# Attention over packed keys and a token-mixing MLP: new routes for the first loads, and a new order

## The chip, the cores and the metric

The kernel runs on one core of a Trainium2 chip. The metric is the device time of one execution in microseconds (us). The core has five engines that work side by side, each through its own list of instructions in order: TensorE (PE, with its weight loads as PEld), VectorE (DVE), ScalarE (ACT), GpSimd (POOL) and SyncE (SP). Transfers between the main memory (DRAM) and the on-chip memory run on 16 DMA engines. Three instruction lists hand out transfers here: SP and ACT feed hardware queues, which copy bytes as they are; GpSimd feeds a software queue, which can also cast float32 to bfloat16 on the way (the casting queue).

## The reference

Inputs: q, k, v of shape (8 batches, 8 heads, 576 tokens, 64), p of shape (8, 8, 32, 64), and three weights of the MLP; all float32.

```python
def sm_attn(qq, kk, vv):
    s = scale * np.matmul(qq, kk.transpose(0, 1, 3, 2))
    s = s - np.max(s, axis=-1, keepdims=True)
    a = np.exp(s)
    a = a / (np.sum(a, axis=-1, keepdims=True) + 1e-09)
    return np.matmul(a, vv)
p_packed = sm_attn(p, k, v)              # 32 packed tokens attend to 576
x = sm_attn(q, p_packed, p_packed)       # 576 tokens attend to 32; heads side by side: (8, 576, 512)
wq, wk = x @ w_q, x @ w_k                # 512 -> 64
W_tok = scale2 * einsum('bsd,btd->bst', wq, wk)
mixed = einsum('bst,btd->bsd', W_tok, x)
out = np.maximum(mixed, 0.0) @ w_out     # (8, 576, 512), float32
```

## The kernel before

The eight batches are independent, and each goes through the same steps. The order of all steps is one text, ORDER (lines 12 to 57): a list of items that a loop at the end of the kernel (line 599) turns into instructions one after the other. An item names a step, the batch, a part of it, after @ the engine (V, A, P for VectorE, ScalarE, GpSimd; S for SP), and after = the banks of the matmul memory. Since every engine runs its own instructions in the order in which they were issued, this text sets for each engine what stands behind what. Waits between engines follow from the data.

The steps of a batch b, in the order in which the data goes through them:

- LD.k, LD.v, LD.q (function load, line 154): the inputs, cast to bf16 on the casting queue. v is two requests (line 173), the others one (lines 176 and 182), q of batches 0 and 7 two halves, r and q (line 179). There are four buffers of each.
- KT (line 255): VectorE's 32 x 32 block transpose of k. S1 (line 263): scores of p against k on TensorE. X1 (line 293): their exponential on ScalarE. TE: a block transpose of that. PV (line 306): times v, 36 matmuls. RC, PP, PT: the division, a mask for the heads, and a transpose, on VectorE.
- QK, QKE, QD: the packed tokens times the small weights (wqk), copied out, and a copy on GpSimd.
- QV: the block transpose of q. S2 (line 373): scores of q against the packed tokens, in parts of the tokens (part 2 is the last 128-token piece, 0 and 1 pairs of pieces, 3 all four). X2 (line 378): exponential. HA (only batch 5, line 388): a first halving of the row sums on GpSimd. RS, RR, AM (lines 394, 399, 405): row sums, reciprocals, and the product on GpSimd (now and then VectorE). AT, AE: transposes on TensorE and their copies.
- WKQ, WE, GM, GE, Y, YE, MX, MR: the token mixing as a chain of matmuls and copies. RL, RLF, RLR: relu. OT (line 540): the output product, four matmuls each; OE, OEF: copies to the output tiles; ST, STF, STH: stores. OT.b.4 is a remainder of two batches together. OH, OEH, STH handle the last piece of batch 7 in halves.

WARM items (line 615) are matmuls on zeros whose results nobody reads. They stand in the first part of the order, the last ahead of MX.1.0 behind the scores S2.2 of batch 2. WARM.n is n units of 128 columns; a third number caps the width of each.

What the change touches stands at the start. p comes as two float32 copies, LD.N0 on ACT's queue and LD.N1 on SP's (line 161), into p32, and is cast by two ScalarE copies, NC (line 239), into pbf. PX (line 246) then transposes it into pT, which S1 of every batch reads. The two small weights come as LD.W0 and LD.W1 (line 164) behind p on the same hardware queues into w32, and GpSimd casts them, WC (line 243). On the casting queue k of batch 0 stands first, in halves: LD.h (line 168) and LD.g (line 157), then v, r, q of batch 0 and k1. SET items prepare constants: the mask, the identity (aff on GpSimd, idb), the ones beside v, the zeros beside aT.

HOLD.v7 (line 567) is a tiny copy on SP's queue which waits until v of batch 7 has landed; the stores on SP stand behind it. GpSimd gives out a few stores itself (ST items with @P).

Of the kernel before, what the change touches and what calls it, by code (L numbers as in the profile page):

```python
# [17 lines left out]
AM.0.2@P WARM.6=7 AT.0.2=7 AE.0.2@A RS.0.0@V RR.0.0@V KT.1.2@V WARM.5=6 S1.1=2,3,0,1 X1.1.0@A AM.0.0@P
RS.0.1@V AT.0.0=6 RR.0.1@V AE.0.0@V TE.1.0@V QD.0@P WARM.2=4 WKQ.0.0=4,5 WKQ.0.2 X1.1.1@A TE.1.1@V AM.0.1@P
AT.0.1=7 LD.q2 PV.1.0=2,3 PV.1.1 WE.0.0@V RC.1@V AE.0.1@A WKQ.0.1 WE.0.1@A WARM.2=6 GM.0=6 LD.k3 PP.1.1@V  # L20
PP.1.0@V PT.1@V QV.1.2@V GE.0@A WARM.1=0 Y.0=0,1 YE.0@A QK.1=4 QKE.1@V WARM.1=7 S2.1.2=2,3 S2.1.1=6,7 X2.1.2@A
RS.1.2@V S2.1.0=0,1 X2.1.1@A LD.O MR.0=4,5 RR.1.2@V AM.1.2@P RLR.0@A KT.2.2@V MX.0.1=2,3 WARM.3=6 AT.1.2=6
X2.1.0@A QD.1@P WARM.1=7 S1.2=4,5,0,1 RL.0.1@A LD.v3 AE.1.2@A MX.0.0=2,3 X1.2.1@A RS.1.0@V RR.1.0@V RS.1.1@V
AM.1.0@P X1.2.0@A TE.2.1@V RR.1.1@V AM.1.1@P TE.2.0@V RL.0.0@A WARM.6=7 AT.1.0=7 AE.1.0@V PV.2.0=0,1 PV.2.1
LD.k4 RC.2@V PP.2.0@V AT.1.1=6 AE.1.1@A LD.q3 LD.v4 WKQ.1.0=4,5 WKQ.1.2 WE.1.0@A PP.2.1@V WKQ.1.1 WE.1.1@A
PT.2@V QK.2=2 QKE.2@A QV.2.2@V LD.q4 WARM.1=3 GM.1=3 QD.2@P GE.1@A WARM.1=7 Y.1=6,7 S2.2.2=0,1 X2.2.2@A
KT.3.2@V S2.2.3=4,5 YE.1@A WARM.1=2 MX.1.0=2,3 X2.2.3@A MX.1.1=0,1 MR.1=6,7 RLR.1@A RS.2.4@V RL.1.0@A RR.2.4@V
# [33 lines left out]
def kernel(  # L61
# [92 lines left out]
    def load(x, eng):  # L154
        a, b = x[0], x[1:]
        if a == "g":
            nc.gpsimd.dma_start(k_in[0][:, 1], pairs(k, 0)[:, 1])
        elif a == "N":
            i, n = int(b), L * Dh // 4
            src = p.rearrange("b (i c) (z l) d -> i (c z) b (l d)", i=2, z=4)  # L160
            (nc.sync if eng == "S" else nc.scalar).dma_start(p32[:, i * n:(i + 1) * n], src[i])
        elif a == "W":
            w = (moe_w_k, moe_w_q)[int(b)].rearrange("(i c j e) m -> (c j) i (e m)", i=2, c=4, e=2)
            (nc.sync if eng == "S" else nc.scalar).dma_start(w32[:, int(b)], w)
        elif a == "O":
            nc.gpsimd.dma_start(wout, moe_w_out.rearrange("(j a) n -> a j n", a=P))
        elif a == "h":
            nc.gpsimd.dma_start(k_in[0][:, 0], pairs(k, 0)[:, 0])
        elif a == "v":
            b = int(b)  # L170
            for i in range(2):
                src = v[b, 4 * i:4 * i + 4].rearrange("c (g r) d -> g c (r d)", r=R)
                nc.gpsimd.dma_start(v_bufs[b % NL][halves(i), 0:7:2], src)  # L173
        elif a == "k":
            b = int(b)
            nc.gpsimd.dma_start(k_in[b % NL], pairs(k, b))
        elif a == "r" or x in ("q0", "q7"):
            b, i = int(b), int(a == "q")
            nc.gpsimd.dma_start(q_in[b % NL][:, i], pairs(q, b)[:, i])
        else:  # L180
            b = int(b)
            nc.gpsimd.dma_start(q_in[b % NL], pairs(q, b))
# [53 lines left out]
    def blocks(o, i):  # L236
        nc.vector.transpose(o, i)  # L237
# [411 lines left out]
```

## Time and profile before

| what | us |
|---|---|
| median of 3 runs (104.53 to 105.03) | 104.9 |
| the profiled execution | 105.18 |
| its span, first to last instruction | 103.4 |
| TensorE busy | 93.2 |
| VectorE busy | 74.0 |
| ScalarE busy | 65.2 |
| GpSimd busy | 53.2 |

A page of the profile gives busy times and groups of instructions by line of the kernel; out<-in are the names of the tiles. Some tiles share memory at the start: p32, pbf, w32 and the warm tile all appear as "o". The timeline gives start, duration, engine, line, operation, and in brackets how long the engine had stood idle before it, and which engine, line or DMA ended that. The chain of waits gives start, duration and work of the chain that ended last. The granted TensorE clock was 1.000 throughout.

### The profile page before, as it was taken

What the parts mean: (1) busy time and instruction counts of PE and PEld (TensorE: products, weight loads), DVE (VectorE), ACT (ScalarE), POOL (GpSimd) and SP (SyncE); (2) the same over time, 40 slices, a digit from 0 to 9 for tenths busy, and PEclk for the clock granted to TensorE, in tenths of its full rate; (3) what the DMA queues carried; (4) which work ended last, traced back from release to release, by engine and by line L of the source; (5) the groups of instructions that cost most, each with busy time, mean ns of one, the idle gap of its engine ahead of it and who ended that gap; (6) DMA issues with size and microseconds to landing.
All of it is one profiled execution on the core that took longest, in us unless ns stands there. A gap on an engine that the chain in (4) does not pass through costs nothing.

```text
span 103.4 us, 3594 instructions
## 1 busy us (share of the span) xinstructions
PE 93.2 (90%) x1531; PEld 57.3 (55%) x1546; DVE 74.0 (72%) x139; ACT 65.2 (63%) x112; POOL 53.2 (51%) x83
## 2 busy tenths in 40 slices
PE   5996999999979988999988899999999999999950
PEld 3895455567537744664547445684557763744430
DVE  4055366979597869696999959989899898138540
ACT  1340406164866697367975979899999698587320
POOL 5973890693379725943049289507667408200000
PEclk9999999999999999999999999999999999999999
DMA  1999999999999999999999999999999999965994
GB/s 27 233 229 207 213 210 206 210 213 209 209 213 209 207 209 211 213 210 209 213 208 210 216 207 206 213 210 210 208 314 406 413 422 403 410 266 227 388 361 163
DMA packets 13632, 25.13 MB, mean 243 GB/s; under 512 B 1073, under 2 KB 6449, under 8 KB 13617
## 3 DMA queue, kind: packets, MB, share of 16 engines
q0 software_dynamic: 10000, 17.30, 84.3%
q1 hardware_dynamic: 3056, 7.08, 18.0%
q10 hardware_dynamic: 560, 0.52, 2.0%
q8 instruction: 12, 0.20, 0.7%
q14 instruction: 4, 0.02, 0.1%
HBM read 30.15 MB, written 9.44 MB: 383 GB/s over the span
## 4 chain that ended last, share of the span: by engine, by line
PE 54%; DMA 22%; DVE 6%; ACT 6%; POOL 5%; issue 2%; SPq 1%; ACTq 0%; DVEq 0%; POOLq 0%
PE ps L540 27%; DMA k_sb<-in_k_dram 14%; DMA o<-in_moe_w_q_dram 8%; PE ps L315 4%; PE ps L373 3%; PE ps L419 3%; PE ps L446 3%; DVE kT L237 3%; ACT e L378 2%; PE ps L492 2%; PE ps L467 2%; PE ps L441 2%; POOL a L405 2%; PE ps L615 2%; PE ps L282 2%
## 5 line engine op out<-in xcount | busy, mean ns | idle before, releaser
L405 POOL TENSOR_TENSOR a<-e,rr 128x256 bf16<-128x256 f32 (+2 forms) x18 | 19.6, 1098 | 24.1 <-DVE rr L399 16.9
L540 PE MATMUL ps<-wout,relu 128*128 128x512 bf16 x112 | 29.2, 380 | 1.0 <-issue 0.5
L615 PE MATMUL ps<-o 128*128 128x128 f32 (+3 forms) x86 | 22.2, 397 | 1.3 <-DVE o L135 1.2
L540 PEld LDWEIGHTS <-relu 128*128 128x128 bf16 x124 | 10.6, 98 | 12.0 <-issue 1.8
L615 PEld LDWEIGHTS ps<-o 128*128 128x128 f32 x86 | 13.2, 213 | 6.0 <-issue 3.9
L128 ACT ACTIVATE o<-ps 128x1024 f32<-128x1024 f32 (+1 forms) x13 | 12.5, 959 | 4.2 <-PE ps L540 3.9
L293 ACT ACTIVATE e1T<-ps 128x576 bf16<-128x576 f32 x16 | 9.7, 653 | 7.2 <-PE ps L282 7.2
L394 DVE TENSOR_REDUCE rs<-e 128x16 f32<-128x512 f32 (+2 forms) x13 | 11.0, 850 | 2.9 <-ACT e L378 2.8
L378 ACT ACTIVATE e<-ps 128x256 f32<-128x256 f32 (+2 forms) x19 | 11.3, 625 | 2.3 <-PE ps L373 2.2
L237 DVE STREAM_TRANSPOSE kT<-k_sb 128x1152 uint32<-128x1152 uint32 (+1 forms) x9 | 11.0, 1218 | 2.1 <-DMA k_sb<-in_k_dram 2.1
L503 ACT ACTIVATE relu<-ps 128x1024 bf16<-128x1024 f32 (+1 forms) x12 | 11.1, 957 | 1.3 <-PE ps L492 1.2
L237 DVE STREAM_TRANSPOSE qT<-q_sb 128x1152 uint32<-128x1152 uint32 (+1 forms) x10 | 11.0, 1108 | 0.7 <-DMA q_sb<-in_q_dram 0.7
L173 POOL DMA_DIRECT2D v_sb<-in_v_dram x16 | 10.2, 648 | 0.3 <-POOL v_sb L206 0.3
L128 ACT ACTIVATE aT<-ps 128x128 bf16<-128x128 f32 (+2 forms) x12 | 6.4, 548 | 5.8 <-PE ps L419 4.4
L237 DVE STREAM_TRANSPOSE e<-e1T 128x288 uint32<-128x288 uint32 x16 | 7.1, 458 | 1.6 <-ACT e1T L293 1.3
L315 PE MATMUL ps<-v_sb,e 64*64 64x192 bf16 x288 | 7.5, 245 | 0.0
L128 ACT ACTIVATE wkq<-ps 128x448 bf16<-128x448 f32 (+1 forms) x8 | 5.8, 728 | 2.3 <-PE ps L446 1.4
L132 DVE COPY o<-ps 128x512 f32<-128x512 f32 (+2 forms) x7 | 5.4, 768 | 2.6 <-PE ps L540 1.9
L446 PE MATMUL ps<-aT,pqk 128*128 128x256 bf16 (+1 forms) x48 | 6.8, 246 | 0.0
L315 PEld LDWEIGHTS <-e 64*64 64x64 bf16 x288 | 5.9, 107 | 1.3 <-DVE e L237 0.9
L373 PE MATMUL ps<-ppT,qT 64*128 64x64 bf16 x320 | 6.5, 190 | 0.0
L441 PE MATMUL ps<-pqk,aT 128*128 128x64 bf16 x80 | 6.2, 194 | 0.3 <-ACT aT L128 0.2
(69 smaller groups left out, 134.5 us busy)
## 6 DMA issues: line engine op xcount, KB each, us to landing
v_sb<-in_v_dram POOLq DMA_DIRECT2D x16, 288.0 KB, 11.2
out_dram<-o SPq DMA_DIRECT2D x8, 512.0 KB, 6.5
k_sb<-in_k_dram POOLq DMA_DIRECT2D x7, 576.0 KB, 12.9
q_sb<-in_q_dram POOLq DMA_DIRECT2D x6, 576.0 KB, 13.3
out_dram<-o POOLq DMA_DIRECT2D x5, 512.0 KB, 9.1
out_dram<-o SPq DMA_DIRECT2D x5, 256.0 KB, 2.4
q_sb<-in_q_dram POOLq DMA_DIRECT2D x4, 288.0 KB, 11.3
out_dram<-orem SPq DMA_DIRECT2D x4, 256.0 KB, 6.1
```

The source lines that it names most:

```text
L128: nc.scalar.activation(o, i, COPY)
L173: nc.gpsimd.dma_start(v_bufs[b % NL][halves(i), 0:7:2], src)
L237: nc.vector.transpose(o, i)
L293: nc.scalar.activation(e1T[:, x], T["s1", b][x].rearrange("a c m -> a m c"), EXP, scale=scale)
L315: nc.tensor.matmul(T["pv", b][halves(cc), i], lhsT, rhs, start=n == 0, stop=n == R - 1, skip_group_check=True)
L378: nc.scalar.activation(e2[:, t0:t1].rearrange("a t (i y n) -> a y (t i) n", i=2, y=2), T["s2", b, c].rearrange("a y t i n -> a y (t i) n") ...
L394: nc.vector.tensor_reduce(rs[:, t0 * H:t1 * H], src, axis=AX, op=ADD)
L405: e.tensor_tensor(a2[:, t0:t1].rearrange("a t i (u l) -> a (t i u) l", l=L), e2v(b, c), T["rr", b][:, t0 * H:t1 * H].to_broadcast((P, (t1 ...
L446: nc.tensor.matmul(o, pqk[:, i, Dl:], aT[:, i, c0:c1], start=i == 0, stop=i == 1)
L503: nc.scalar.activation(o, i, RELU)
L540: nc.tensor.matmul(ps, lhsT, wout[:, j, :], start=j == 0, stop=j == NJ - 1)
L615: nc.tensor.matmul(bank(int(bk), [w]), warm[:, 0:P], rhs, start=True, stop=True)
```

## The change

- k of batch 0: the first half (LD.h, casting queue) becomes LD.H, a float32 copy on SP's hardware queue into h32 (in an output tile not yet in use), and a ScalarE copy HC casts it into k_in. The second half, LD.g, stays on the casting queue.
- p: LD.N0 and LD.N1 move to the head of the casting queue and land in bf16 in pbf. NC goes.
- The small weights: LD.W0 and LD.W1 move to the casting queue, W0 behind q and r of batch 0, W1 behind k1. WC goes.
- The mask is set on VectorE instead of GpSimd.
- ORDER is new from end to end. The requests of the casting queue were h g v0 r0 q0 k1 v1 q1 k2 v2 q2 k3 O v3 k4 q3 v4 q4 k5 v5 k6 q5 v6 q6 k7 v7 q7 r7 (O is w_out) and become N0 N1 g v0 q0 r0 W0 k1 W1 k2 v1 q1 v2 q2 O k3 v3 k4 q3 v4 q4 k5 v5 q5 k6 v6 q6 k7 v7 q7 r7. The last WARM stands ahead of QK.2. GpSimd's stores go from five (0.0, 1.1, 3.1, 4.1, 3.0) to two (1.1, 3.1), the others go on SP's queue.

```diff
 ORDER = """
-LD.N0@A LD.N1@S SET.warm@V SET.v0@V SET.aT0@V SET.aT1@V SET.aT2@V SET.idf@V LD.W0@A LD.W1@S SET.tab@A LD.h0
-LD.g0 LD.v0 LD.r0 LD.q0 LD.k1 NC.1@A PX.1@V NC.0@A PX.0@V SET.aff@P SET.idb@V KT.0.0@V KT.0.1@V SET.mask@P
-WARM.4=0 WARM.22.128=0 S1.0=0,1,2,3 X1.0.1@A TE.0.1@V X1.0.0@A TE.0.0@V SET.v2@P WARM.8=4 PV.0.0=4,5 PV.0.1
-RC.0@V PP.0.0@V PP.0.1@V PT.0@V WC.0@P QV.0.0@V WC.1@P WARM.6=6 QK.0=6 SET.v3@P QV.0.1@V QKE.0@A WARM.4=7
...
+LD.H@S SET.warm@V SET.v0@V SET.aT0@V SET.aT1@V SET.aT2@V SET.idf@V SET.tab@A LD.N0 LD.N1 LD.g0 LD.v0 LD.q0
+LD.r0 LD.W0 LD.k1 SET.aff@P SET.mask@V HC@A PX.0@V KT.0.0@V PX.1@V KT.0.1@V SET.idb@V WARM.4=0 WARM.18.128=0
+S1.0=0,1,2,3 X1.0.0@A TE.0.0@V X1.0.1@A TE.0.1@V WARM.8=4 PV.0.0=4,5 PV.0.1 RC.0@V PP.0.1@V PP.0.0@V QV.0.1@V
+PT.0@V LD.W1 QV.0.0@V WARM.12=6 S2.0.2=6,7 S2.0.0=0,1 X2.0.2@A RS.0.2@V RR.0.2@V LD.k2 SET.v1@P LD.v1
+S2.0.1=2,3 LD.q1 X2.0.0@A RS.0.0@V AM.0.2@P WARM.6=5 AT.0.2=5 X2.0.1@A RR.0.0@V AM.0.0@P WARM.5=4 AT.0.0=4
+AE.0.2@A AE.0.0@A RS.0.1@V RR.0.1@V AM.0.1@P QK.0=6 QKE.0@A KT.1.2@V QD.0@P S1.1=0,1,2,3 AT.0.1=7 WKQ.0.0=4,5
+X1.1.1@A WKQ.0.2 X1.1.0@A AE.0.1@V WKQ.0.1 TE.1.1@V WE.0.0@A WE.0.1@A WARM.3=6 GM.0=6 SET.v2@P GE.0@A WARM.1=2
+Y.0=2,3 YE.0@A TE.1.0@V KT.2.2@V S1.2=0,1,4,5 X1.2.0@A MR.0=6,7 RLR.0@V MX.0.1=2,3 MX.0.0=0,1 RL.0.1@V
+X1.2.1@A TE.2.1@V PV.1.0=6,7 PV.1.1 RC.1@V PP.1.0@V PP.1.1@V RL.0.0@A LD.v2 PT.1@V WARM.7=4 QK.1=4 LD.q2
+QKE.1@A QV.1.2@V WARM.4=5 S2.1.2=2,3 X2.1.2@A S2.1.0=0,1 S2.1.1=6,7 LD.O LD.k3 SET.v3@P X2.1.0@A TE.2.0@V
+WARM.5=5 PV.2.0=4,5 PV.2.1 LD.v3 LD.k4 RS.1.2@V RR.1.2@V RS.1.0@V QD.1@P AM.1.2@P AT.1.2=2 RR.1.0@V AM.1.0@P
...
+RC.4@V RR.3.4@V AM.3.3@P PP.4.0@V OT.2.1 OE.1.0@A PP.4.1@V PT.4@V QK.4=3 QV.4.2@V AM.3.2@P QKE.4@V AT.3.3=2
...
+AT.4.2=7 AE.4.2@A MR.3=4,5 RLR.3@A QV.5.2@V PT.5@V MX.3.1=0,1 RL.3.1@A MX.3.0=6,7 RL.3.0@A AT.4.3=3 OT.3.4=2
+S2.5.2=4,5 OEF.3.4@A X2.5.2@A S2.5.3=0,1 X2.5.3@A AE.4.3@V KT.6.2@V QD.4@P WKQ.4.0=6,7 WKQ.4.2 WKQ.4.1
...
+OE.3.0@A HA.5@P RS.5.4@V LD.v7 LD.q7 RR.5.4@V LD.r7 QK.5=4 QKE.5@A PV.6.0=0,1 PV.6.1 MX.4.1=6,7 RL.4.1@A
...
+RLF.7.1.0@A OEF.7.4@A ST.7.4 OT.7.0=4 OEF.7.0@A STF.7.0 OT.7.1=5 OEF.7.1@A STF.7.1 OT.7.2=1 OEF.7.2@A OH.7.0=7
+STF.7.2 OEH.7.0@A OH.7.1=6 STH.7.0 OEH.7.1@A STH.7.1@A
...
         elif a == "N":
             i, n = int(b), L * Dh // 4
             src = p.rearrange("b (i c) (z l) d -> i (c z) b (l d)", i=2, z=4)
-            (nc.sync if eng == "S" else nc.scalar).dma_start(p32[:, i * n:(i + 1) * n], src[i])
+            nc.gpsimd.dma_start(pbf[:, i * n:(i + 1) * n], src[i])
         elif a == "W":
             w = (moe_w_k, moe_w_q)[int(b)].rearrange("(i c j e) m -> (c j) i (e m)", i=2, c=4, e=2)
-            (nc.sync if eng == "S" else nc.scalar).dma_start(w32[:, int(b)], w)
+            nc.gpsimd.dma_start(wqk[:, :, int(b)].rearrange("a i e m -> a i (e m)"), w)
...
-        elif a == "h":
-            nc.gpsimd.dma_start(k_in[0][:, 0], pairs(k, 0)[:, 0])
+        elif a == "H":
+            nc.sync.dma_start(h32, pairs(k, 0)[:, 0])
...
-    def WC(x, eng, bk):
-        copy(eng, wqk[:, :, x].rearrange("a i e m -> a i (e m)"), w32[:, x])
+    def HC(eng, bk):
+        copy(eng, k_in[0][:, 0], h32)
```

More of the change, by code (lines that the diff above doesn't have):

```diff
@@ L18 @@
[L18 to L27, printed above, removed]
@@ new lines @@
+WARM.1=0 QK.2=0 QKE.2@A AT.1.1=1 WKQ.1.0=6,7 WKQ.1.2 QV.2.2@V AE.1.1@A WKQ.1.1 WE.1.1@A S2.2.2=4,5 X2.2.2@A
+S2.2.3=2,3 X2.2.3@A WE.1.0@V GM.1=0 OT.0.0=6,7 GE.1@V Y.1=4,5 OT.0.1 RS.2.4@V YE.1@A MR.1=0,1 OE.0.0@A
+RR.2.4@V MX.1.0=2,3 KT.3.2@V RLR.1@V OT.0.2=4,5 LD.q3 LD.v4 RL.1.0@A OT.0.3 OE.0.1@V S1.3=6,7,2,3 X1.3.0@A
+TE.3.0@V AM.2.2@P AT.2.2=0 X1.3.1@A TE.3.1@V OT.1.4=1 AM.2.3@P AE.2.2@A AT.2.3=6 AE.2.3@A MX.1.1=4,5 OEF.1.4@V
+PV.3.0=2,3 RL.1.1@A PV.3.1 RC.3@V PP.3.0@V PP.3.1@V KT.4.2@V QD.2@P WKQ.2.0=0,1 WKQ.2.1 WKQ.2.2 WE.2.2@A
@@ new lines @@
+OE.3.0@A HA.5@P RS.5.4@V LD.v7 LD.q7 RR.5.4@V LD.r7 QK.5=4 QKE.5@A PV.6.0=0,1 PV.6.1 MX.4.1=6,7 RL.4.1@A
+MX.4.0=2,3 RL.4.0@A AM.5.2@P RC.6@V AM.5.3@P OT.3.2=4,5 PP.6.0@V OT.3.3 AT.5.2=0 PP.6.1@V PT.6@V QK.6=1
+QV.6.2@V AE.5.2@A HOLD.v7 OE.3.1@V ST.1.1@P QD.5@P QKE.6@A QD.6@P S2.6.2=6,7 X2.6.2@A S2.6.3=2,3 X2.6.3@A
+MR.4=0,1 AT.5.3=6 AE.5.3@A OT.4.0=4,5 KT.7.2@V RS.6.4@V RR.6.4@V ST.0.0 OT.4.1 WKQ.5.0=2,3 ST.1.4 WKQ.5.2
+ST.2.1 WKQ.5.1 RLR.4@A ST.3.1@P OE.4.0@A WE.5.2@A S1.7=6,7,0,1 AM.6.3@V X1.7.1@A TE.7.1@V OT.4.2=4,5 ST.4.0
```

55 lines of the change are left out of this document (19 added, 36 removed).

## The prediction

> **What bounds the kernel now.** I read the page first (shares, slices, groups), then busy time by stretch, the DMA queues by stretch, the timeline of the first 30 us, and last the timeline wherever a step stands at a comparable spot in both orders. From the page:
>
> ```profile
> span 103.4 us, 3594 instructions
> ...
> PE 93.2 (90%) x1531; PEld 57.3 (55%) x1546; DVE 74.0 (72%) x139; ACT 65.2 (63%) x112; POOL 53.2 (51%) x83
> ...
> DMA  1999999999999999999999999999999999965994
> ...
> L615 PE MATMUL ps<-o 128*128 128x128 f32 (+3 forms) x86 | 22.2, 397 | 1.3 <-DVE o L135 1.2
> ```
>
> TensorE looks 90% busy, but 22.2 us of its 93.2 are L615, the dummy WARM matmuls: real work is 71 us. The DMA slices are full from the second slice to the 36th. By stretch (start and end, length, busy time of PE, PEld, DVE, ACT, POOL, then clock, DMA share, GB/s):
>
> ```profile
> 35.00:40.00 5.00, 4.22 (x101) 2.70 (x99) 3.66 (x5) 4.15 (x9) 1.12 (x4) 1.00 1.22 210
> ...
> 50.00:60.00 10.00, 8.71 (x175) 5.17 (x176) 9.49 (x16) 8.05 (x13) 4.65 (x6) 1.00 1.14 211
> 60.00:70.00 10.00, 9.79 (x220) 6.14 (x220) 8.27 (x15) 8.49 (x14) 6.43 (x10) 1.00 1.14 209
> ...
> 80.00:90.00 10.00, 9.89 (x173) 6.02 (x165) 7.37 (x17) 8.05 (x17) 4.07 (x6) 1.00 1.03 412
> ```
>
> There are two regimes. The last WARM of the order stands behind the first scores of batch 2, near 36.6 us; until then TensorE waits for data. After it TensorE has a backlog and hardly pauses (9.79 and 9.89 of 10 us). What pauses remain: 0.78 us in 35 to 40 and 1.29 us in 50 to 60. So the end follows from how much real work is done when WARM stops, plus the holes behind it. I therefore follow one quantity through the new order: how far TensorE is ahead of (-) or behind (+) the old order at equal work.
>
> The loads write bf16 at a steady 212 GB/s (20 to 30 us), so one k, q or v of a batch (0.59 MB in bf16) takes 2.8 us. At the start the queues wake at different times; the three rows are 20 to 30, 2.0 to 2.5 and 4.0 to 4.5 us:
>
> ```profile
> DMA packets 1236, 2.12 MB, mean 212 GB/s; under 512 B 69, under 2 KB 589, under 8 KB 1234
> ```
> ```profile
> q10 hardware_dynamic: 34, 0.07, 98.1%
> ```
> ```profile
> q0 software_dynamic: 14, 0.03, 33.5%
> ```
>
> **Step 1, the start of batch 0.** Timeline of before:
>
> ```profile
> 0.74 0.71 SPq L161 DMA_DIRECT2D o<-in_p_dram  x1
> ...
> 1.26 0.73 POOL L168 DMA_DIRECT2D k_sb<-in_k_dram  x1 [0.82 <-POOLq L633]
> ...
> 1.99 0.55 POOL L157 DMA_DIRECT2D k_sb<-in_k_dram  x1
> ...
> 5.74 1.15 ACT L128 ACTIVATE o<-o 128x512 bf16<-128x512 f32 x2 [2.17 <-DMA o<-in_p_dram]
> ...
> 6.40 1.17 DVE L237 STREAM_TRANSPOSE pT<-o 128x256 uint32<-128x256 uint32 x2 [4.28 <-ACT o L128]
> ...
> 12.63 0.94 PE L315 MATMUL ps<-v_sb,e 64*64 64x192 bf16 x36
> ...
> 13.94 0.61 DVE L323 SCALAR_TENSOR_TENSOR pp<-ps,rec,mask 128x128 bf16<-128x128 f32 x2
> ...
> 14.58 0.31 DVE L237 STREAM_TRANSPOSE ppT<-pp 128x128 uint32<-128x128 uint32 x1
> 14.82 1.39 DVE L237 STREAM_TRANSPOSE qT<-q_sb 128x576 uint32<-128x576 uint32 x2
> ...
> 16.39 0.78 PE L373 MATMUL ps<-ppT,qT 64*128 64x64 bf16 x40
> ```
> ```profile
> 7.54 0.73 DVE L237 STREAM_TRANSPOSE kT<-k_sb 128x576 uint32<-128x576 uint32 x1
> ...
> 9.47 0.78 DVE L237 STREAM_TRANSPOSE kT<-k_sb 128x576 uint32<-128x576 uint32 x1 [1.20 <-DMA k_sb<-in_k_dram]
> ...
> 10.31 0.48 PE L282 MATMUL ps<-kT,pT 32*32 32x288 bf16 x30 [0.85 <-DVE kT L237]
> ```
>
> The first hardware queue moves bytes at 2.0 us, the casting queue at 4.0, though it was issued at 1.26. The second half of k of batch 0 lands last (9.47) and holds the scores until 10.31. In the changed kernel the first half goes out at 0.74 on SP and has the DMA engines alone until 4: I take it as landed at 5.4 (p landed at 5.74 the same way), and ScalarE's cast of 1152 columns at 1.3 us (two of 512 took 1.15). Two p requests (0.13 MB each in bf16, 0.6 us each) then stand ahead of the second half, issued at 2.5 instead of 1.99, but the first half (1.4 us at 212 GB/s) and the small weights no longer compete. So p lands near 6.1 and 6.7, the second half at 8.3 (bounds 7.9, the p time saved twice, and 9.0, a slow start of the queue). VectorE's chain (PX 0.6, KT 0.73, PX 0.6) is done at 8.1, so KT.0.1 runs 8.3 to 9.05 and the scores go at 9.15, 1.15 us earlier. PV.0 follows at 11.5, QV.0.1 now runs before PT.0 (0.73 + 0.31 us), S2.0 at 15.3: **-1.1** (bounds -0.5 to -1.6). ScalarE loses NC, GpSimd loses WC and the mask: hidden by the waits seen here, cost nothing. The mask's memsets now on VectorE lie in its 4.28 us wait. Fewer WARM units (18 for 22) keep TensorE out of the way.
>
> The Trainium skill (DMA: Bandwidth & Descriptors, Issuing engines are not separate DMA queues) says transfers of all issuing engines share the same DMA engines, and several issuers save only issue time. By that the first half would gain one issue slot, 0.73 us by the row of 1.26, and this term would be -0.7. The rows at 2.0 and 4.0 speak for more: the hardware queue runs while the casting one is still silent.
>
> **Step 2, the loads change places.** Now k2 is requested ahead of v1 and q1. From the chain of waits, then the timeline:
>
> ```profile
> 13.49 14.35 DMA k_sb<-in_k_dram
> ```
> ```profile
> 24.45 1.34 DVE L237 STREAM_TRANSPOSE qT<-q_sb 128x1152 uint32<-128x1152 uint32 x1
> ...
> 25.89 0.77 PE L373 MATMUL ps<-ppT,qT 64*128 64x64 bf16 x40
> ```
> ```profile
> 29.29 0.49 PE L282 MATMUL ps<-kT,pT 32*32 32x288 bf16 x32 [0.65 <-DVE kT L237]
> ```
>
> In before k2 closes the set {p, small weights, k0 v0 q0, k1 v1 q1, k2} and lands at 13.49 + 14.35 = 27.84. In the changed kernel q1 closes the same set, so q1 lands at 27.8 (earlier by at most step 1's 1.1). QV.1 (1.34) ends at 29.35 and S2.1 starts at 29.4, against 25.89. In return k2 lands two transfers earlier, 22.2, and S1.2 runs near 24.1 instead of 29.29. Count at 29.4: the new order has S1.2 (0.49) and MX.0.0 (0.3) more, S2.1 (0.86) and one small transpose (0.1) less. The lead is gone: **+0.2** (term +1.3; if q1 comes 1.1 earlier, the term is +0.2).
>
> **Step 3, w_out ahead of k3.** Step by step from S2.1 the new order reaches the end of S2.2 at 36.3 with GM.1 and Y.1 (0.5) still to do; before it was 36.6. That is the same +0.2. Behind it before stalls:
>
> ```profile
> 35.56 1.38 DVE L237 STREAM_TRANSPOSE kT<-k_sb 128x1152 uint32<-128x1152 uint32 x1 [0.38 <-DMA k_sb<-in_k_dram]
> 35.82 0.71 POOL L182 DMA_DIRECT2D q_sb<-in_q_dram  x1 [0.77 <-DMA k_sb<-in_k_dram]
> ...
> 38.80 0.75 PEld L540 LDWEIGHTS <-rem 128*128 128x128 bf16 x4 [0.50 <-DMA wout<-in_moe_w_out_dram]
> 39.01 1.02 PE L540 MATMUL ps<-wout,rem 128*128 128x512 bf16 x3 [0.45 <-ACT relu L503]
> ```
> ```profile
> 48.84 0.88 PE L373 MATMUL ps<-ppT,qT 64*128 64x64 bf16 x40
> ```
>
> Now w_out is requested before k3, lands about 35, and OT.0 fills TensorE while k3 comes (38, 2.5 us later than 35.56: S1.3 waits behind four OT anyway). The waits of 0.50 and part of 0.45 go. I reach S2.3, which hangs on q3 (same bytes ahead of it in both), at 49.1 against 48.84, with 0.7 us more work done: **-0.4** (term -0.6; bounds 0 and -1.0, both waits in full).
>
> The row at 35.82 shows a limit: q4 is the 23rd casting request and waits for the 15th, k3. So GpSimd waits for the request eight back. With two more requests ahead this moves the waits; k6 and v6 will hold GpSimd until about 50.5, in front of AM.3, which is not ready before 52. No cost, unless AM.3 comes earlier.
>
> **Step 4, 49 to 69 us.**
>
> ```profile
> 53.02 2.48 POOL L405 TENSOR_TENSOR a<-e,rr 128x1024 bf16<-128x1024 f32 x2 [4.55 <-DVE rr L399]
> ...
> 54.98 0.62 PE L419 MATMUL ps<-idb,a 128*128 128x128 bf16 x8 [0.21 <-POOL a L405]
> ```
> ```profile
> 68.46 0.11 PEld L477 LDWEIGHTS <-g 64*64 64x64 bf16 x4
> 68.47 0.25 PE L477 MATMUL ps<-pp,g 64*64 64x128 bf16 x4
> ```
>
> Behind S2.3 TensorE waits for AM.3 in both orders: AT.3 at 55.2 against 54.98, but one more OT (0.86) is done: -0.6 (term -0.2). From there to Y.4 the same work is left apart from that OT, 12.7 us; I find holes: S2.5 waits for PT.5, which now stands behind QV.5 (0.35), and three of 0.1 to 0.15 at AT.3.2, S1.5 and PV.5. Y.4 at 68.6 against 68.47: **+0.15** (term +0.75; bounds 0 and +1.3, the 1.29 of holes seen in 50 to 60).
>
> **Step 5, the last loads and the tail.**
>
> ```profile
> 63.21 1.26 POOL L173 DMA_DIRECT2D v_sb<-in_v_dram  x2
> ...
> 69.69 1.56 POOL L388 TENSOR_TENSOR h<-e 128x640 f32<-128x640 f32 x1 [3.57 <-ACT e L378]
> ```
>
> Now HA.5 stands in front of v7, q7 and r7 on GpSimd. S2.5 and its exponentials are done near 66.5, HA.5 (1.56) at 68.1, so v7 goes out 5 us later than at 63.21. What is queued ahead of it (k7 last) drains near 69, and a request takes up to 2.7 us to move bytes (4.0 less 1.26), so the DMA engines can pause for up to 1.8 us. SP's stores wait behind HOLD.v7 and start that much later. TensorE has a backlog then, so most is hidden; and all six last evictions are on ScalarE (before half were on VectorE). I take **+0.45** (bounds 0 and +1.8).
>
> The sum: -1.1 + 1.3 - 0.6 - 0.2 + 0.75 + 0.45 = +0.6. The profiled execution took 105.18 us (span 103.4 and 1.78 around it) and becomes 105.8; the median of the runs, 104.9, is 0.28 lower, so 105.5.
>
> The skill's table (same page, Specifications) says pieces under 512 B cost a read-modify-write; the cast small weights are written in 256 B pieces. As an estimate from that page, doubling 0.13 MB would add 0.6 us to every later landing; no row here shows such writes, and it is not in the sum.
>
> **Rivals.**
> (a) Slower, 105.5 (forecast): the lead of batch 0 is eaten by q1's place, and new holes decide. For it: 27.84 and the count at 29.4. Chance 0.42.
> (b) Faster, 104.0: the lead survives. It does if q1 lands 1.1 us earlier than 27.8, as the whole set starts earlier, and step 4 has half its holes: -1.1 + 0.2 - 0.6 - 0.2 + 0.4 + 0.4 = -0.9. For it: S2.1 hangs on q1 alone. Against: the rate, 212 GB/s, is full from 9 us on, so only bytes moved before 9 us help. It decides from a landing before 27. Chance 0.28.
> (c) No change, 104.9: steps 1 to 4 as worked out (+0.15) and the late v7 hidden. Chance 0.2.
> (d) Clearly slower, 106.7: the pause of 1.8 us reaches the last stores, which wait for the SP queue behind HOLD.v7: +0.15 + 1.8. Against: DMA has slack at the end (slices 6, 5). Chance 0.1.
>
> **How the numbers follow.** About 0.5% is what a measurement of this kernel can tell from no change: 0.5 us. Cases (a) and (d) are slower, but a fifth of (a) lies within 0.5%: slower 0.44, same 0.28, faster 0.28. The range reaches from (b) to (d): 103.9 to 106.7; the forecast's own range is 104.9 to 106.2.
>
> **What would show it.** Step 1: the second kT of batch 0 near 8.3 and the first S2 near 15.3. Step 2: the third qT (batch 1) waits for its DMA until 27.8. Step 3: no wait for wout. Step 4: a wait of TensorE for ppT near 64. Step 5: a dip in the DMA slices near 69 and v7 issued near 68. I am wrong if q1 lands before 27, or if TensorE's holes between 50 and 70 stay below 1 us.

## The result, and the profile after

The changed kernel takes 105.03 us (median of 20 runs, 104.5 to 105.89), the kernel before, run beside it on the same chip, 104.51 us (20 runs, 104.15 to 105.03). The ratio is 1.0045, with a 95% interval of 1.0024 to 1.0066: the change costs about 0.47 us. That is just inside the 0.5% within which the prediction speaks of no change, and the interval reaches across that line. The forecast, 105.5, was a slower kernel by 0.6; its range holds the time. Medians here and below take in all runs, ratios leave out runs that lie more than 1.5% above the fastest of their kernel.

The profiled execution took 105.89 us, the longest of its 20 runs. The page after:

```profile
span 104.0 us, 3588 instructions
...
PE 95.6 (92%) x1534; PEld 56.7 (55%) x1534; DVE 72.5 (70%) x143; ACT 66.8 (64%) x112; POOL 52.2 (50%) x76
...
DMA  3999999999999999999999999999999999984974
...
L609 PE MATMUL ps<-o 128*128 128x128 f32 (+3 forms) x74 | 22.5, 454 | 1.2 <-DVE o L134 1.2
```

The dummy WARM matmuls (now L609) still take 22.5 us, so real work is 73 us against 71. The first DMA slice is busier (3 against 1). Busy time of each engine by stretch, first after, then before (columns as in the prediction):

```profile
50.00:55.00 5.00, 4.47 (x68) 2.44 (x68) 4.14 (x9) 4.22 (x6) 2.79 (x3) 1.00 1.14 210
65.00:70.00 5.00, 4.65 (x106) 2.36 (x102) 2.90 (x8) 4.06 (x7) 4.19 (x6) 1.00 1.12 212
80.00:85.00 5.00, 4.45 (x106) 2.90 (x97) 3.41 (x8) 3.76 (x9) 0.00 (x0) 1.00 1.03 412
```
```profile
50.00:55.00 5.00, 4.15 (x61) 2.12 (x62) 4.69 (x10) 3.78 (x5) 1.98 (x2) 1.00 1.13 209
65.00:70.00 5.00, 4.95 (x151) 3.56 (x150) 4.42 (x8) 4.41 (x8) 1.43 (x4) 1.00 1.12 212
80.00:85.00 5.00, 4.94 (x130) 3.54 (x122) 4.34 (x11) 4.13 (x10) 1.21 (x2) 1.00 1.03 415
```

The first column of busy time is TensorE's. The new order pauses less at 50 to 55 us, but has pauses at 65 to 70 (0.35 us against 0.05) and at 80 to 85 (0.55 against 0.06), where the old one had hardly any. Step 4 of the prediction had looked for its holes earlier, from AT.3 near 55 us to S2.5 near 64.

The timeline of the changed kernel, the rows that answer to the steps:

```profile
4.36 1.16 ACT L127 ACTIVATE k_sb<-o 128x1152 bf16<-128x1152 f32 x1 [2.13 <-DMA o<-in_k_dram]
...
8.47 0.78 DVE L235 STREAM_TRANSPOSE kT<-k_sb 128x576 uint32<-128x576 uint32 x1 [0.94 <-DMA k_sb<-in_k_dram]
...
15.36 0.78 PE L367 MATMUL ps<-ppT,qT 64*128 64x64 bf16 x40
...
27.61 1.38 DVE L235 STREAM_TRANSPOSE qT<-q_sb 128x1152 uint32<-128x1152 uint32 x1 [0.33 <-DMA q_sb<-in_q_dram]
...
29.05 0.78 PE L367 MATMUL ps<-ppT,qT 64*128 64x64 bf16 x40
...
48.66 0.87 PE L367 MATMUL ps<-ppT,qT 64*128 64x64 bf16 x40
...
54.80 0.62 PE L413 MATMUL ps<-idb,a 128*128 128x128 bf16 x8
...
65.57 1.56 POOL L382 TENSOR_TENSOR h<-e 128x640 f32<-128x640 f32 x1 [3.23 <-ACT e L372]
...
68.45 1.29 PE L309 MATMUL ps<-v_sb,e 64*64 64x192 bf16 x36 [0.27 <-ACT y L478]
...
75.16 0.64 SPq L566 DMA_DIRECT2D touch<-v_sb  x1
...
83.92 0.60 ACT L127 ACTIVATE orem<-ps 128x512 f32<-128x512 f32 x1 [0.96 <-PE ps L367]
...
84.56 0.41 PE L330 MATMUL ps<-wqk,ppT 64*64 64x128 bf16 x8 [0.48 <-ACT orem L127]
...
99.08 1.04 PE L571 MATMUL ps<-wout,relu 128*128 128x256 bf16 x8
```

Two rows are new kinds of wait. At 68.45 PV.6 (the product of v and the exponentials of batch 6) waits. At 84.56 QK.7 waits until a remainder of the output (orem) is copied out of the PSUM bank that QK.7 writes; and the chain of waits shows what that copy waited for:

```profile
76.75 7.07 DMA out_dram<-orem
83.92 0.04 ACT orem L127
84.08 0.34 issue
84.41 0.60 ACT e L372
85.05 0.25 PE ps L471 x4
```

The tile orem has two buffers, and the copy for batch 5 had to wait until the store of batch 1, given out at 76.75, had read the same buffer. The last product starts at 99.08, 4.92 us before the span's end; before it was 98.52 and 4.88. So nothing was lost behind the last product.

### The profile page after: what moved, and what is told of

Its sections match the earlier page's. It is cut to its first block, busy times and chain, and to the rows that moved or that the text cites. A ratio compares the mean times of both kernels' runs of the same rounds, so it can differ in the third digit from the quotient of the medians.

```text
span 104.0 us, 3588 instructions
## 1 busy us (share of the span) xinstructions
PE 95.6 (92%) x1534; PEld 56.7 (55%) x1534; DVE 72.5 (70%) x143; ACT 66.8 (64%) x112; POOL 52.2 (50%) x76
## 4 chain that ended last, share of the span: by engine, by line
PE 42%; DMA 29%; ACT 10%; DVE 5%; POOL 5%; issue 5%; ACTq 0%; POOLq 0%
PE ps L534 24%; DMA q_sb<-in_q_dram 22%; DMA out_dram<-orem 7%; PE ps L367 4%; POOL a L399 2%; PE ps L413 2%; ACT o L127 2%; PE ps L309 2%; ACT relu L497 2%; ACT e1T L287 2%; PE ps L486 2%; ACT wkq L127 2%; PE ps L440 2%; DVE rs L388 1%; PE ps L461 1%
## 5 line engine op out<-in xcount | busy, mean ns | idle before, releaser
L534 PE MATMUL ps<-wout,relu 128*128 128x512 bf16 x124 | 30.5, 380 | 0.5 <-ACT relu L497 0.5
L609 PE MATMUL ps<-o 128*128 128x128 f32 (+3 forms) x74 | 22.5, 454 | 1.2 <-DVE o L134 1.2
L609 PEld LDWEIGHTS ps<-o 128*128 128x128 f32 x74 | 12.9, 235 | 6.3 <-issue 4.6
L127 ACT ACTIVATE o<-ps 128x1024 f32<-128x1024 f32 (+2 forms) x16 | 13.2, 839 | 3.7 <-PE ps L534 3.6
L497 ACT ACTIVATE relu<-ps 128x1024 bf16<-128x1024 f32 (+1 forms) x13 | 12.0, 956 | 1.0 <-PE ps L486 1.0
L127 ACT ACTIVATE aT<-ps 128x128 bf16<-128x128 f32 (+2 forms) x12 | 5.8, 482 | 4.1 <-PE ps L408 2.5
L127 ACT ACTIVATE wkq<-ps 128x896 bf16<-128x896 f32 (+1 forms) x9 | 6.6, 752 | 1.2 <-PE ps L440 0.9
L175 POOL DMA_DIRECT2D k_sb<-in_k_dram x7 | 5.1, 733 | 3.8 <-DMA q_sb<-in_q_dram 3.0
L367 PEld LDWEIGHTS <-qT 64*128 64x128 bf16 x320 | 5.4, 94 | 2.9 <-DVE qT L235 1.6
```

The costliest lines, as they stand in the source:

```text
L127: nc.scalar.activation(o, i, COPY)
L367: nc.tensor.matmul(ps[:, y, t - t0, i], lhsT, rhs, start=e == 0, stop=e == 1)
L497: nc.scalar.activation(o, i, RELU)
L534: nc.tensor.matmul(ps, lhsT, wout[:, j, :], start=j == 0, stop=j == NJ - 1)
L609: nc.tensor.matmul(bank(int(bk), [w]), warm[:, 0:P], rhs, start=True, stop=True)
```

## The experiments

**The same kernels again.** One execution of a kernel can stand half a microsecond from the next, so the first question is which rows are the usual ones.

> The kernel before, unchanged, for a second profiled execution. The first one took 105.18 us where the median of its runs is 104.5, so something in it was 0.6 us slower than usual. Theory T (the difference of usual runs lies where TensorE is starved, ahead of PV.2): PV.7 and all behind it stand some 0.3 to 0.6 us earlier than in the first profile (79.78). Rival: only the last stores differ, and PV.7 stands where it stood.

> The changed kernel, unchanged, for a second profiled execution. The first took 105.89 us where the median is 105.0. Theory W (the wait of OT.5.4's copy for the store ST.1.4 is there in every execution): TensorE is idle for 0.4 us or more ahead of QK.7, near 84 us. Rival V (it comes and goes with the stores, and was not the cause of the usual 0.5 us): no such hole, span near 103.1.

> The changed kernel, unchanged, for a third profiled execution. As for the second: theory W expects the hole ahead of QK.7 again, rival V expects it in some executions only.

The execution of after_b took 107.22 us, with a granted clock of 0.91 in its first 20 us, so only what lies behind 60 us is used of it. before_b took 104.51 us, after_c 105.4. From the timelines of before_b, then of after_c:

```profile
16.06 0.77 PE L373 MATMUL ps<-ppT,qT 64*128 64x64 bf16 x40
...
27.19 1.38 DVE L237 STREAM_TRANSPOSE kT<-k_sb 128x1152 uint32<-128x1152 uint32 x1
...
48.17 0.88 PE L373 MATMUL ps<-ppT,qT 64*128 64x64 bf16 x40
...
67.79 0.25 PE L477 MATMUL ps<-pp,g 64*64 64x128 bf16 x4
...
67.90 0.94 PE L315 MATMUL ps<-v_sb,e 64*64 64x192 bf16 x36
...
97.85 1.04 PE L577 MATMUL ps<-wout,relu 128*128 128x256 bf16 x8
```
```profile
27.66 1.38 DVE L235 STREAM_TRANSPOSE qT<-q_sb 128x1152 uint32<-128x1152 uint32 x1 [0.78 <-DMA q_sb<-in_q_dram]
...
68.50 0.60 PE L309 MATMUL ps<-v_sb,e 64*64 64x192 bf16 x19 [0.27 <-ACT y L478]
69.65 0.60 PE L309 MATMUL ps<-v_sb,e 64*64 64x192 bf16 x17 [0.55 <-issue]
...
98.69 1.04 PE L571 MATMUL ps<-wout,relu 128*128 128x256 bf16 x8
```

Two things follow. The execution of before on which the prediction was built is 0.67 us later than this one at every step from 35 us to the end (48.84 and 48.17, 98.52 and 97.85), and two things differ ahead of that: the start of batch 0 (S2.0 by 0.33 us) and k2, which is waited for until 27.86 there and is there by 27.19 here. S1.2 stands right behind the transpose of k2 and moves by the same 0.67. The order is fixed, so what comes late there moves all that follows. And the wait of QK.7 for orem is not in after_c (nor in after_b), while the one of PV.6 is in both, with a second stall of 0.55 in the middle of PV.6 for which the profile names no releaser.

From here on I compare with before_b. The lead at a step is how much earlier TensorE starts it, plus the difference of the TensorE work done by then, from the two orders and the durations of rows (at S2.3 the new order has one OT and the small MR.2 more done, and QK.3 not yet: +0.68 us, so 48.66 gives 48.17 - 48.66 + 0.68 = +0.19; PV.6 starts 0.55 later with QK.5, 0.35 us, already done: -0.20). Ahead is positive:

```
step       at (us)   before   after   after_c   e1      e12
S2.0       16.06     -0.33    +0.35   +0.75     +0.53   +0.56
S2.2       35.13     -0.68    -0.47   -0.53     -0.25   -0.22
S2.3       48.17     -0.67    +0.19   +0.09     +0.41   +0.41
PV.5       59.71     -0.67    +0.36   +0.30     +0.59   +0.61
Y.4        67.79     -0.68    +0.08   +0.03     +0.30   +0.34
PV.6       67.90     -0.68    -0.20   -0.25     +0.03   +0.16
S1.7       74.41     -0.67    -0.58   -1.10     -0.39   -0.55
PV.7       79.11     -0.67    -0.18   -0.70     +0.01   -0.15
Y.6        83.90     -0.67    -1.15   -0.72     -0.01   -0.17
last OH    97.85     -0.67    -1.23   -0.84     -0.13   -0.29
```

The lead won at the start is gone at S2.2, comes back at S2.3, holds through the middle, and is lost behind Y.4. The rest of the experiments ask why, at these two places.

**The shared remainder tile (e1_orem_own).** OT.5.4's remainder gets memory of its own:

```diff
-            copy(eng, new("orem", b // 2, [P, D], fp32, bufs=2), T["otf", b, t])
+            if b == 5:
+                T["orem", 2] = k_in[0].rearrange("a i n -> a (i n)").bitcast(fp32)[:, 0:D]
+            else:
+                new("orem", b // 2, [P, D], fp32, bufs=2)
+            copy(eng, T["orem", b // 2], T["otf", b, t])
```

> The changed kernel, with a tile of its own for the remainder of batches 4 and 5 (OT.5.4), so that its copy no longer waits for the store ST.1.4 to land. Theory W (the lead of the first 70 us is lost to this wait, near 83 to 85 us): the hole of TensorE ahead of QK.7 goes, the output matmuls end 0.5 to 1.0 us earlier, 104.1 to 104.5 us where the changed kernel takes 105.0. Rival S (the stores and the late loads set the end): the wait goes but the time stays within 0.2 us.

Measured: 104.99 us (12 runs, 104.59 to 106.43), ratio 1.0037 (1.0013 to 1.0062). The wait for orem is gone, the time is not: the ratio was 1.0045 with the wait's cause in place. So the largest hole of the first profile, and the chain through it, belong to that one execution and not to the usual loss. PV.6 still waits:

```profile
27.04 1.34 DVE L235 STREAM_TRANSPOSE qT<-q_sb 128x1152 uint32<-128x1152 uint32 x1
...
68.22 1.32 PE L309 MATMUL ps<-v_sb,e 64*64 64x192 bf16 x36 [0.26 <-ACT y L478]
...
97.98 1.04 PE L575 MATMUL ps<-wout,relu 128*128 128x256 bf16 x8
```

**The last loads ahead of HA.5 (e2_v7first).**

```diff
- OE.3.0@A HA.5@P RS.5.4@V LD.v7 LD.q7 RR.5.4@V LD.r7 QK.5=4
+ OE.3.0@A LD.v7 LD.q7 LD.r7 HA.5@P RS.5.4@V RR.5.4@V QK.5=4
```

> The changed kernel, with the last requests (v7, q7, r7) ahead of HA.5 on GpSimd. Theory W: the DMA engines had no pause, so nothing is gained: 104.9 to 105.2 us, with HA.5 and AM.5 some 2.4 us later and perhaps a small loss. Rival S (step 5 of the prediction: late requests delay HOLD.v7 and the stores): v7 lands earlier, the stores start earlier, 0.4 us or more is gained, 104.6 us or less.

Measured: 105.11 us, ratio 1.0056 (1.0032 to 1.008). Nothing is won, and v7 was not late to begin with: SP's copy that holds the stores back until v7 is there starts at 75.16 in the changed kernel and at 74.88 here; before, it was this row:

```profile
74.93 0.60 SPq L572 DMA_DIRECT2D touch<-v_sb  x1
```

Nor do the DMA engines pause: their slices from 66 to 76 us in the changed kernel (40 slices of 0.25 us) are all but one at 90% or more.

```profile
DMA  9999989999999999999999999999999999999999
GB/s 207 217 203 278 212 166 221 203 203 212 203 230 203 221 184 212 207 180 221 198 194 221 198 207 207 203 226 241 221 175 235 198 189 226 198 240 192 276 231 284
```

**Work ahead of PV.6 (e3_pv6fill, e10_orem_pv6, e12_pv6only).** In the changed order PV.6 stands right behind Y.4 and QK.5 and waits in every execution. What it reads are v and the transposed exponentials. The profile names those in e9 (the second row below) and in the others a copy of ScalarE, y, that PV.6 doesn't read. But the two transposes end 0.05 to 0.06 us ahead of PV.6 in each of them (in after_c, the first row, at 67.43 + 1.02 = 68.45, and PV.6 starts at 68.50), so they are what is late.

```profile
67.43 1.02 DVE L235 STREAM_TRANSPOSE e<-e1T 128x288 uint32<-128x288 uint32 x2
```
```profile
68.12 0.94 PE L309 MATMUL ps<-v_sb,e 64*64 64x192 bf16 x36 [0.27 <-DVE e L235]
```

e3 moves a product that is ready, OT.3.2, in front of it:

```diff
- ... QK.5=4 QKE.5@A PV.6.0=0,1 PV.6.1 ... AM.5.3@P OT.3.2=4,5 PP.6.0@V OT.3.3
+ ... QK.5=4 QKE.5@A OT.3.2=4,5 PV.6.0=0,1 PV.6.1 ... AM.5.3@P PP.6.0@V OT.3.3
```

> The changed kernel, with the output product OT.3.2 moved ahead of PV.6, which stood waiting for its block transposes near 68.4 us. The hole of 0.3 us ahead of PV.6 and the slow half of PV.6 go. Theory W: the wait for the store of ST.1.4 ends at the same time whatever happens at 68 us, so the end stays: 104.9 to 105.1 us. Rival P (each hole of TensorE counts by itself): 0.4 us faster, 104.6 us.

Measured: 106.09 us, ratio 1.0155 (1.0131 to 1.0179), 1.1 us worse than the changed kernel, which neither theory expected. The fill brought a wait of its own, since its banks 4 and 5 take in the bank of QK.5, which has to be copied out first:

```profile
69.19 1.02 PE L534 MATMUL ps<-wout,relu 128*128 128x512 bf16 x4 [1.46 <-ACT pqk L127]
...
73.61 0.78 PE L367 MATMUL ps<-ppT,qT 64*128 64x64 bf16 x40 [0.63 <-DVE qT L235]
```

e10 (with e1's own tile) and e12 (without it) take QK.5 out of the way as well:

```diff
- ... LD.r7 QK.5=4 QKE.5@A PV.6.0=0,1 PV.6.1 ... OT.3.2=4,5 PP.6.0@V OT.3.3 AT.5.2=0 PP.6.1@V PT.6@V QK.6=1
+ ... LD.r7 OT.3.2=4,5 PV.6.0=0,1 PV.6.1 ... PP.6.0@V OT.3.3 AT.5.2=0 PP.6.1@V PT.6@V QK.5=0 QKE.5@A QK.6=1
```

> The kernel of e1_orem_own with OT.3.2 ahead of PV.6, and QK.5 moved behind PV.6 to bank 0, so that OT.3.2 finds its banks free (in e3_pv6fill it waited 1.5 us for QK.5's copy). Theory H (with the store's wait gone, the holes near 68 us count at the end): PV.6 no longer waits, 0.3 to 0.6 us are gained over e1_orem_own, 104.4 to 104.7 us, about the kernel before or a little under it. Rival (the instruction stall inside PV.6 moves elsewhere, or QK.5's later place costs as much): 105.0 us.

> The changed kernel with the move of OT.3.2 and QK.5 of e10_orem_pv6, but with the shared tile for the remainders. Theory V (the wait for the store ST.1.4 shows in some executions only, the hole ahead of PV.6 in all): as e10_orem_pv6, 104.6 to 104.8 us. Theory W (the store's wait is usual and swallows what is gained at 68 us): as the changed kernel, 105.0 us, and TensorE is idle ahead of QK.7.

Measured: e10 104.68 us, ratio 1.0003 (0.9976 to 1.0029); e12 104.68 us, ratio 1.0002 (0.9978 to 1.0027). In e12, PV.6 has no wait in front:

```profile
68.60 1.31 PE L309 MATMUL ps<-v_sb,e 64*64 64x192 bf16 x36
...
98.14 1.04 PE L571 MATMUL ps<-wout,relu 128*128 128x256 bf16 x8
```

So both kernels with this one move are level with the kernel before, and the five that keep PV.6 where the change put it and differ little otherwise (after, e1, e2, e9, e11) stand at 1.0032 to 1.0056. The medians put the move at 0.3 to 0.4 us, most of the change's cost. It is the grouping that carries this: the intervals of e12 and e1 overlap, and in single profiles the loss from Y.4 to PV.6 shrinks only from 0.27 to 0.18 (e12 in the table), and S2.6 gets a wait (0.39 us, for q transposed) in return. No version beat the kernel before.

What the profiles do show is that PV.6 itself takes longer. Its 36 matmuls take 0.94 us in both executions of before and in e8, e9 and e11, 1.29 in after, 1.32 in e1, 1.59 in e2, and 1.75 and 1.76 in after_c and after_b, the stop in the middle counted in. All of these but before have the same work from PV.6 to S1.7. It takes 7.56 or 7.57 us in e8, e9 and e11, then 7.90, 7.94, 8.21, 8.37 and 8.38 in the order above: the excess of PV.6 to within 0.01 us. It shows at the end too: from Y.4 to the last product it is 30.06 us in before_b, 30.12 in e11, 30.36 in e9, 30.49 in e1, 30.76 in e2 and 30.93 in after_c (31.37 in after, which has the wait for orem besides).

The stop is tied to a place in TensorE's list of instructions. It comes behind the 19th weight load of PV.6, and in e10 and e12, where the four matmuls of OT.3.2 stand in front in place of the eight of QK.5, behind the 23rd. From e12:

```profile
68.60 0.47 PEld L309 LDWEIGHTS <-e 64*64 64x64 bf16 x23 [0.42 <-DVE e L235]
69.40 0.30 PEld L309 LDWEIGHTS <-e 64*64 64x64 bf16 x13 [0.32 <-issue]
```

The DMA view has a queue for instructions, and one block comes on it shortly before. This row is after_c, 67.3 to 67.4 us:

```profile
q8 instruction: 1, 0.02, 60.1%
```

In the seven executions with a slow PV.6 the loads go on 2.2 to 2.5 us after such a block (in after_c at 69.65). In e8, e9 and e11 TensorE reaches the same place 2.6 to 3.1 us after it and does not stop. That fits a TensorE that waits for its next instructions; no run changes this alone, so it is not shown as the cause. Nor do the profiles show what e10 and e12 win: the stop is in both (0.26 and 0.37 us).

**The start (e4_routes, e9_warm22, e11_warm12).** e4 keeps the old order and has the new routes alone (k's first half on the hardware queue, p and the small weights on the casting queue):

```diff
-LD.N0@A LD.N1@S ... LD.W0@A LD.W1@S SET.tab@A LD.h0 LD.g0 LD.v0 LD.r0 LD.q0 LD.k1 NC.1@A PX.1@V NC.0@A PX.0@V ... KT.0.0@V KT.0.1@V
+LD.H@S ... SET.tab@A LD.N0 LD.N1 LD.g0 LD.v0 LD.r0 LD.q0 LD.W0 LD.W1 LD.k1 HC@A PX.0@V KT.0.0@V PX.1@V KT.0.1@V
```

> The order of before, with the new routes of the first loads alone (first half of k of batch 0 on SP's hardware queue and cast by ScalarE, p first in the casting queue, small weights cast there behind q of batch 0, no NC and WC). If the routes are worth step 1: S2 of batch 0 near 15.4 us, 1.0 earlier. Theory (the gain of the routes survives when the order is not changed): k2 lands up to 0.3 us earlier and the end is 0.2 to 0.8 us earlier than before, 103.7 to 104.3 us. Rival (the middle hangs on the loads' rate, which is the same): k2 still lands at 27.8 and the time is that of before, 104.5 us.

Measured: 104.97 us, ratio 1.0029 (1.0 to 1.0058): no gain. From its timeline:

```profile
14.64 0.41 PE L331 MATMUL ps<-wqk,ppT 64*64 64x128 bf16 x8 [0.64 <-DMA wqk<-in_moe_w_q_dram]
...
16.05 0.77 PE L368 MATMUL ps<-ppT,qT 64*128 64x64 bf16 x40
...
19.09 1.38 DVE L236 STREAM_TRANSPOSE kT<-k_sb 128x1152 uint32<-128x1152 uint32 x1 [0.81 <-DMA k_sb<-in_k_dram]
```

PV.0 starts at 11.57, as early as in the changed kernel (11.63). But in the old order QK.0 stands in front of S2.0 and needs w_q, which now comes last of the first loads: S2.0 starts at 16.05, as in before_b. S2.0 is earlier in the changed kernel only because routes and order go together (QK.0 moved behind S2.0).

e9 and e11 were to take the start's gain back with more dummy matmuls, ahead of S1.0 and ahead of PV.0:

```diff
-WARM.4=0 WARM.18.128=0
+WARM.4=0 WARM.22.128=0
```
```diff
-TE.0.1@V WARM.8=4 PV.0.0=4,5
+TE.0.1@V WARM.12=4 PV.0.0=4,5
```

> The changed kernel with 22 narrow WARM matmuls at the start instead of 18, so that the first scores of batch 0 start about 1.2 us later, as late as in the kernel before (10.3 us). Theory L (the middle hangs on the landing of q1, not on batch 0): S2 of batch 0 is 1 us later, but QV.1, PV.2 and everything from 30 us on stand where they stood, and the time stays at 105.0 us within 0.2. Rival E (the earlier start is worth what step 1 said): the end is 0.8 to 1.2 us later, 106 us.

> The changed kernel with 12 units of WARM ahead of PV.0 instead of 8 (e9_warm22 did not delay the first scores at all: they started at 9.0 us). PV.0 starts at about 12.4 us instead of 11.3 to 11.6, and S2 of batch 0 about 0.9 us later, as late as in the kernel before. Theory L (from 25 us on the order hangs on the landing of q1, not on batch 0): S2.1 and PV.2 stand where they stood (31.0 us), and the time stays within 0.25 us of the changed kernel's 105.0. Rival E (step 1's gain reaches the end): 0.8 to 1.1 us slower, 105.9 us.

e9 missed its aim: S1.0 still starts at 9.00, and the time is 104.91 (1.0032, 1.0003 to 1.0061), as before the edit. e11 does delay, by 0.87 us: from S1.0 to PV.0 it is 3.19 us (9.87 to 13.06) against 2.32 in e1 (9.22 to 11.54). Yet its median is 104.97 us (1.0043, 1.0018 to 1.0069), that of e1. So 0.87 of the 1.1 us that step 1 won is worth less than these runs can tell, some 0.3 us. The profiled execution of e11 (105.91 us, of a median of 104.97) shows where that ends: its S1.0 came late by itself, by another 0.65, S2.0 started at 16.70, and then the chain of batch 0 and not q1 was last:

```profile
28.55 1.34 DVE L235 STREAM_TRANSPOSE qT<-q_sb 128x1152 uint32<-128x1152 uint32 x1
```

It has no wait in front. From S2.0 to this row it is 11.85 us (16.70 to 28.55), in e1, where there is no wait either, 11.86 (15.18 to 27.04). So the chain needs 11.86 us, q1 is there at times by 26.8 (e3, whose transpose starts then without a wait) and at times only at 27.66, and a start ahead of some 14.9 to 15.8 is waited away.

**w_out behind k3 (e8_orem_o_late).** e1's kernel, with step 3 undone:

```diff
- S2.1.1=6,7 LD.O LD.k3
+ S2.1.1=6,7 LD.k3 LD.O
```

> The kernel of e1_orem_own with w_out requested behind k3 instead of ahead of it, as in the kernel before. If step 3 holds (the lead in the middle comes from w_out's place): OT.0 waits for w_out until about 37.5 us, TensorE stands 1 us or more, the lead of 0.6 us at PV.5 turns into a lag, and the time is 0.5 to 1.0 us above e1_orem_own (105.5 to 106.0 us). Rival (w_out's place is covered, since S2.3 hangs on q3 anyway): within 0.2 us of e1_orem_own.

Measured: 107.47 us (6 runs, 106.22 to 109.55); the ratio, 1.019 (1.0142 to 1.0237), rests on three of them (106.22, 106.49 and 107.0), 1.5 us above e1 and more than the 0.5 to 1.0 expected. The profiled execution is one of the others (107.94), so its times are not compared, only its wait is read:

```profile
38.08 1.06 PE L534 MATMUL ps<-wout,relu 128*128 128x512 bf16 x4 [1.97 <-DMA wout<-in_moe_w_out_dram]
```

In the new order the four OT stand in front of S1.3, so TensorE stops for w_out as a whole. The place of w_out is worth more here than in the old order (0.50 and part of 0.45).

## Why the prediction came out as it did

The sum was +0.6 us; the runs give +0.47 (0.25 to 0.69). The forecast of 105.5 stands 0.47 above the 105.03 measured, and most of that is the level: the three runs of before had a median of 104.9, the twenty beside the changed kernel 104.51. Set on 104.51 the sum gives 105.1. But most of the chance was on slower by over 0.5%, and 0.45% came: q1's place ate the lead, as in rival (a), with an end that counts as no change, as in rival (c). The step that failed is step 5: its +0.45 was to come from late last loads that hold back the stores, and the runs showed no pause of the DMA engines and v7 landed about as before (HOLD.v7 at 75.16 against 74.93); what was lost was lost in PV.6. Step 4 had its holes about 0.45 too large. That the sum is near what was measured is luck in this part: PV.6, no term of the sum, filled the gap that steps 4 and 5 left. Step by step, with what was predicted as the running sum (behind is +) and what the table shows against before_b:

- **Step 1 (-1.1): right in place, and in size within its bounds (S2.0 is 0.7 to 1.4 earlier, by the pair of executions).** The second kT of batch 0 at 8.47 (8.3 predicted), S2.0 at 15.36 (15.3), and 14.96 to 15.39 in the other kernels with this start (without after_b, and e11, which delays it); before, 16.39 and 16.06. Not seen: QK.0, which I left out of this term, is still to do there, so the lead is only 0.35 to 0.75. The first half was cast from 4.36 on and not from 5.4. The second kT came 1.0 earlier in the pair of the prediction (9.47 to 8.47), but before_b has it at 8.90, and the kernels with this start have it between 7.87 and 9.03. The Trainium skill (DMA: Bandwidth & Descriptors, Issuing engines are not separate DMA queues) says that several issuers save only the time of issuing, from which the prediction estimated -0.7; these rows do not tell that from -1.1.
- **Step 2 (+1.3, running sum +0.2): right.** (Its 29.35 for the end of QV.1 is a slip, 27.8 and 1.34 are 29.15; S2.1 started at 29.05.) q1 closes the set that k2 closed and is waited for until 27.61 and 27.66 (27.8 predicted). At S2.2 the kernel is 0.22 to 0.53 behind. e11 bears out that the start's lead dies here. The Trainium skill (same page, Specifications) has a read-modify-write for pieces under 512 B; the 0.6 us on every later landing that the prediction estimated from it is not seen: the set is complete between 26.8 and 27.66 in the kernels with these loads, and by 27.19 and at 27.86 in before.
- **Step 3 (-0.6, running sum -0.4): right.** From S2.2 to S2.3 the lead rises by 0.62 to 0.66 in every column after the change; S2.3 stands at 48.66 (49.1). e8 shows the price of its absence.
- **Step 4 (-0.2 and +0.75, running sum +0.15): the term was mis-sized.** To PV.5 the lead rises by 0.17 to 0.21, as predicted. From AT.3 to Y.4 I had 0.75 of holes; measured are 0.30 (AT.3 at 54.80 against 54.31 with one OT, 0.87, more done is +0.38; Y.4 is +0.08), and Y.4 starts at 67.71 and not 68.6. The wait for PT.5 near 64 that I looked for is not there. The largest holes of the step are these, in the changed kernel:

```profile
52.54 1.89 PE L534 MATMUL ps<-wout,relu 128*128 128x512 bf16 x8 [0.51 <-ACT relu L497]
...
57.55 0.48 PE L276 MATMUL ps<-kT,pT 32*32 32x288 bf16 x32 [0.32 <-DVE kT L235]
```

  before_b has a wait of 0.28 for kT at the place of the second (S1.5), and 0.37 and 0.21 ahead of it: the 12.7 us that I took for the same work already held the old holes, and I added the new ones to them. From 50 to 64 us TensorE pauses for 0.97 us after and for 0.86 in before_b. So at Y.4 the kernel was level or ahead (0.03 to 0.34), and not 0.15 behind.
- **Step 5 (+0.45): the mechanism wrong, the size about right by luck.** v7 went out at 67.07, 3.9 us later than before, but the DMA engines did not pause, and HOLD.v7 stands at 75.16 against 74.93. The six evictions on ScalarE cost nothing (4.92 us from the last product to the end, against 4.88). I had HA.5 done at 68.1 and v7 out after that; HA.5 ran at 65.57. The loss lies in a place that I had no row for: PV.6 right behind Y.4, which waits 0.27 for its exponentials and then takes up to 0.82 longer. e10 and e12 bring 0.3 to 0.4 back by moving work there.

Rival (b) fell although its condition, and with it a sign of being wrong, was met at times: q1 was there by 26.98 in e2 and by 26.80 in e3 (its transpose starts then, without a wait). What I had not seen is that the chain of batch 0, 11.86 us, then ends at the same time: both have to be earlier for the lead to live. Rival (d) fell with the late stores (its own sum gives 106.85 and not 106.7). One reading of the page was off without weight: the DMA slices are full to the 35th and not the 36th.

Open is what makes PV.6 stop, beyond the time at which the block of instructions comes, and why the medians of e10 and e12 are lower although their profiled executions have the stop. Open too is why QK.7 meets the late store in one execution only.

## What to carry to other kernels

A load that arrives earlier is worth only what the next landing leaves of it: work out which set of bytes closes the stage behind, and if that set is the same, the gain ends there (1.1 us won at 15 us, nothing left at 35). When an order is rewritten, ask of every step which stands directly behind another whether its input can be ready, and put ready work there, after a look at whose banks it takes: the same move cost 1.1 us with the wrong banks and won 0.3 to 0.4 with the right ones. And before a hole in one profile is believed, look for it in a second execution: the largest hole here (QK.7 behind a store) was in one of them alone.

## What the runs showed of the hardware

- The same set of bytes lands at times that differ by 0.7 us or more between executions of one kernel (k2 before: 27.86 and by 27.19) or of kernels with the same loads (q1 after: by 26.8 to 27.66), and with a fixed order the whole rest can shift by that: 0.67 us at every later step of before.
- A hardware queue with the DMA engines to itself until 3.4 us finished 0.59 MB of float32 reads by 4.36 us, 3.6 us after its issue at 0.74; I had taken 5.4, from p's landing at 5.74.
- A store of a remainder took 7.07 us from issue to release while the DMA engines were full (76.75 to 83.82), and a tile of two buffers made that a wait of TensorE (0.48 us).
- A run of 36 matmuls of one kind can stop in its middle for 0.21 to 0.76 us (by its weight loads) with no releaser named, in all seven executions at the same place in TensorE's list and 2.2 to 2.5 us behind a block on the instruction queue.
- A casting request waited until the one eight requests back had landed, as the prediction read from its row at 35.82: in the changed kernel k4 for q1 (0.91 us idle, at 27.87) and k6 for q3 (2.07 us, at 47.37).
